# Rebuilding the opening of a fused cosformer attention and SwiGLU kernel: loads, order of the first heads, first FFN products

## The chip, the core and the metric

The kernel runs on one core of one Trainium2 chip. TensorE (PE) multiplies, with its weight loads (PEld) beside the products; VectorE (DVE), ScalarE (ACT) and GpSimd (POOL) do the elementwise work; SyncE (SP) and POOL issue most of the DMAs. The metric is device time in microseconds: 299.17 us in the median of three runs before the change (298.46 to 299.66). All times inside a run are counted from the start of its profiled span.

## What is computed

Linear attention with cosine weights feeds a gated FFN (cut to what matters):

```
# q, k, v: [8 batches, 8 heads, 576 positions, 64]; theta = pi/2 * pos / 576
phi(x) = concat(relu(x) * cos(theta), relu(x) * sin(theta))          # 128 features
kv  = einsum('bhsf,bhsd->bhfd', phi(k), v);   z = sum_s phi(k)
x   = (phi(q) @ kv) / (phi(q) @ z + 1e-6)                            # 4608 tokens x 512
g   = x @ w_gate;  val = x @ w_val                                   # 512 -> 1536
out = (g * sigmoid(g) * val) @ w_out                                 # 1536 -> 512
```

Inputs and output are fp32 in HBM; the kernel multiplies in bf16 and fp16.

## The kernel before

The 4608 tokens make 72 rows of 64 positions and so 36 token tiles of 128 (a tile is two such rows); four tiles make a token group, and nine groups go through the FFN one after the other. A batch of q, k or v is held as `[128, 4, 9, 64]`: 64 partitions for each of two heads, four groups `g` of two heads, nine slots `c`, 64 channels. The slot `c` of q belongs to one half of a token tile, so tile 0 needs slots 0 and 1, tile 1 slots 2 and 3, and so on, of all heads; k and v are needed whole, for all nine slots, before a head's `kv` is known.

Two regimes stand one behind the other.

- **The opening** treats batch 0 and the first half of the gate and value products of token group 0 (blocks `fc` 0 to 5 of 12). Its order is written out by hand in the string `words` (from L510), each word an instruction group that is put on its engine's queue in that order: `rk` relu of k, `kv` the product of k and v by pairs of head groups (`kv_first`, L315), `kvo` its eviction to SBUF, `tq` turning q on PE (`turn_q`, L351), `qr` relu of the turned q, `qw` its copy times tan(theta) (L360), `a` the product of q with kv for a token tile (`a_tile`, L372), `den`, `rec`, `x` the division (L388, L397, L401), `xt` and `xc` the turning of x on PE and its copy to `xT` (L418, L323), `G` and `V` the gate and value products (`ffn_mm`, L438), `s` silu (L445), `m` the product of the two (L450), `WG` and `WV` sums of weights that the later Strassen-like blocks use. A digit after the letter is a token tile or an `fc` block, what stands behind the point is the half (0, 1) or the pair of token tiles (01, 23). `z` puts products of zeros on PE.
- **The planned part** is everything after the words. Each piece of work is a `Job` with durations, dependencies and due times; a list scheduler (`order_once`) puts them in order at build time. Its inputs are constants: release times of loads (`LOADED`, `W_AT`, `WO_AT`), the moment at which each engine is taken to come free (`BUSY_AT`), and a list of seeds (`SEEDS`), one per 10 us of PE work, that shake the due times. Another seed gives another order of the same jobs.

Loads that bring fp32 to fp32 go through SP (`load_first`, L154) into space that is used for something else later: all of v into `wo_sb`, all of k into `ht`, the first two slots of q into `wt_sb`. They are issued at once, in the order v groups 0 and 1, v groups 2 and 3, q slots 0 and 1, k groups 0 and 1, k groups 2 and 3 slots 0 to 4, k groups 2 and 3 slots 5 to 8. ACT then makes bf16 of v (L461), ACT and DVE of q (L339), and the relu of k makes bf16 on the way (L281, L283). Loads that cast from fp32 to bf16 or fp16 go through POOL: q slots 2 and 3, q slots 4 to 7 (`load_slots`, L129), then the gate and value weights (`load_w`, L269 and L270) in blocks of `fc`: 0, 1, then pairs 2-3, 4-5, 6-7, then k of batch 1, and so on. POOL starts with them behind a one-column copy (`hold`, L467) that waits for the first half of v. Eight POOL loads can be outstanding; the ninth waits for the first to land.

Every PSUM result stands in one of eight banks, which `take` hands out and `give_back` frees.

Of the kernel before, what the change touches and what calls it, by code (L numbers as in the profile page):

```python
# [11 lines left out]
FP32 = mybir.dt.float32  # L12
# [7 lines left out]
def kernel(  # L20
# [112 lines left out]
    QCUT = 2  # L133
# [12 lines left out]

    first = {"q": lodge(G * QCUT * D, FP32).rearrange("p (g c d) -> p g c d", g=G, c=QCUT)}

# [15 lines left out]
    NW = 8  # L164
# [26 lines left out]
    idle_products(40, 16)  # L191
    idle_products(4)
# [30 lines left out]
    tan16 = consts.tile([P, NC + 1], FP16, name="tan16")  # L223
    eps_all = consts.tile([P, NC], FP32, name="eps")
    diag = lodge((NC + 1) * SH, FP16).rearrange("p (c s) -> p c s", c=NC + 1)
    tanT = consts.tile([P, NC + 1, SH], FP16, name="tanT")

    def tangents():
        nc.vector.reciprocal(out=rcos, in_=cs_all[:, :, :, 0])
        nc.vector.tensor_tensor(out=tan16[:, 0:NC], in0=csk[:, :, 1], in1=rcos[:, 0], op=ALU.mult)  # L230
        nc.vector.tensor_copy(out=tan16[:, NC:], in_=tan16[:, 0:1])
        nc.vector.tensor_single_scalar(out=eps_all, in_=rcos[:, 1], scalar=1e-6, op=ALU.mult)

    def tangent_diagonals():
        nc.vector.tensor_tensor(out=diag[0:SH], in0=ident16[0:SH, 0:SH].unsqueeze(1).to_broadcast([SH, NC + 1, SH]),
                                in1=tan16[0:SH].unsqueeze(2).to_broadcast([SH, NC + 1, SH]), op=ALU.mult)

    def tangents_spread():
        st["tan"] = take(2, "tan")
        nc.tensor.matmul(out=st["tan"][:, 0], lhsT=ones[0:SH], rhs=diag[0:SH, 0:NW].rearrange("p c s -> p (c s)"),  # L240
                         start=True, stop=True)
        nc.tensor.matmul(out=st["tan"][:, 1, 0:2 * SH], lhsT=ones[0:SH], rhs=diag[0:SH, NW:].rearrange("p c s -> p (c s)"),
                         start=True, stop=True)

    def tangents_out(eng):
        copy_op(eng, tanT.rearrange("p c s -> p (c s)"),
                st["tan"].rearrange("p b x -> p (b x)")[:, 0:(NC + 1) * SH])
        give_back("tan")
# [40 lines left out]
    def relu_first_k(g, eng, lo=0, hi=NC):  # L289
        relu_op(eng, raw_of(0, "k")[:, g, lo:hi], first["k"][:, g, lo:hi])  # L290

    def vmul(b, g):
        nc.vector.tensor_tensor(
            out=v2s[b == 1][:, g, :, :, 0:D],
            in0=(first if b == 0 and g == 0 else {"v": raw_of(b, "v")})["v"][:, g].unsqueeze(2).to_broadcast([P, NC, 2, D]),
# [29 lines left out]
    def kv_first_out(j, e, eng):  # L325
# [6 lines left out]
    qf = wgs_sb.rearrange("p n c u x -> p (n c u x)")[:, G * NC * 2 * W:G * NC * 2 * W + 4 * J * D].bitcast(  # L332
        BF16).rearrange("p (c j i d) -> p c j i d", c=2, j=J, i=2)
# [3 lines left out]
    def cast_q(c, eng):  # L337
        o = qf[:, c % 2].rearrange("p j i d -> p (j i) d")
        (nc.scalar.copy if eng == "act" else nc.vector.tensor_copy)(out=o, in_=first["q"][:, :, c])  # L339

    def turn_q(t):
        ps = take(1, ("tq", t)).bitcast(BF16).rearrange("p (y e s) -> p y e s", e=2, s=SH)
        for j in range(J):
            for c in range(2):
                y = 2 * j + c
                if t == 0:
                    nc.tensor.transpose(out=ps[:, y].rearrange("p e s -> p (e s)"),
                                        in_=qf[:, c, j].rearrange("p i d -> p (i d)"), identity=ident)
                    continue
# [16 lines left out]
    def a_tile(t, j):  # L366
# [3 lines left out]
        for e in range(2):  # L370
            for w in range(2):
                nc.tensor.matmul(  # L372
                    out=(ps[:, j, 2 * e * D1:2 * (e + 1) * D1] if t == 0 else
# [6 lines left out]
    def a_view(t, ps, ys):  # L380
        if t == 0:
# [3 lines left out]
    def x_den(t, ps, ys=slice(0, 4)):  # L385
        if ys.start == 0:
            st["den", t] = den_all[:, t % 4]
        nc.vector.tensor_scalar(  # L388
# [70 lines left out]
    for g in (0, 1, 2, 3):  # L459
# [3 lines left out]
        if g == 1:  # L463
            tangent_diagonals()
# [1215 lines left out]
```

## Time and profile before

| what | us |
|---|---|
| median of three runs | 299.17 (298.46 to 299.66) |
| the profiled execution, whole | 298.92 |
| its span, first to last instruction | 297.1 |
| PE busy in the span | 291.6 (98%) |
| DVE, ACT, POOL busy | 252.9, 199.4, 67.4 |
| first gate product (L438) starts | 16.10 |
| first product of the planned part (L904) starts | 27.41 |
| last stores issued | 293.17 |

PE's busy time contains 65 products of zeros (L187), 56 of them from 0.99 us on, so that its share says little on the first ten microseconds; the time of the opening is read from what each engine waits for, in the timeline. A line of the timeline is start and duration in us, engine, line, operation, output and input, shapes, count, and in brackets the idle time before it and what ended it.

### The profile page before, as it was taken

The numbers are of one execution on the slowest core, as the hardware profiler recorded it, in microseconds if no ns is written. First come the engines' busy times: TensorE is split into PE (matmuls) and PEld (weight loads), VectorE is DVE, ScalarE is ACT, GpSimd is POOL, SyncE is SP. The second block draws the span as 40 slices with busy tenths as digits, with TensorE's granted clock in tenths as the row PEclk, the third lists the DMA queues.
The fourth block names the chain that finished last, engine by engine and source line by source line (L and its number), as shares of the span: only waits on it lengthen the run. The fifth ranks groups of instructions, "written<-read, shape, count | busy, mean of one in ns | idle before, by whom it ended". The sixth has DMA issues, their size and how long they took to land.

```text
span 297.1 us, 8071 instructions
## 1 busy us (share of the span) xinstructions
PE 291.6 (98%) x3244; PEld 238.9 (80%) x3244; DVE 252.9 (85%) x514; ACT 199.4 (67%) x421; POOL 67.4 (23%) x122
## 2 busy tenths in 40 slices
PE   8999999999999999999999999999999999999994
PEld 4597465776787888898898889888988988888883
DVE  8878997879877999999888997998679868986883
ACT  6564346989559968975699589967465556565630
POOL 6763630003006022220352023200220050002000
PEclk9999999999999999999999999999999999999999
DMA  7999999997989998799996969950460045002025
GB/s 259 232 196 198 202 206 207 199 220 122 190 163 146 226 189 122 148 171 149 159 213 128 196 106 169 163 100 2 109 107 2 0 83 132 2 0 73 0 59 156
DMA packets 71973, 40.89 MB, mean 138 GB/s; under 512 B 48768, under 2 KB 68736, under 8 KB 71936
## 3 DMA queue, kind: packets, MB, share of 16 engines
q0 software_dynamic: 24800, 24.39, 48.9%
q1 hardware_dynamic: 46528, 15.47, 28.9%
q10 hardware_dynamic: 608, 0.52, 0.6%
q8 instruction: 25, 0.41, 0.6%
q14 instruction: 12, 0.10, 0.1%
HBM read 37.75 MB, written 9.44 MB: 159 GB/s over the span
## 4 chain that ended last, share of the span: by engine, by line
PE 94%; DMA 1%; DVE 1%; SPq 1%; issue 1%; ACT 0%
PE banks L977 44%; PE banks L1142 23%; PE banks L1052 5%; PE banks L1262 4%; PE banks L438 4%; PE banks L904 4%; PE banks L187 3%; PE banks L716 2%; PE banks L785 2%; DMA xT<-x 1%; SPq L747 1%; PE banks L779 1%; PE banks L372 1%; PE banks L1310 0%; PE banks L315 0%
## 5 line engine op out<-in xcount | busy, mean ns | idle before, releaser
L1111 POOL DMA_DIRECT2D out_dram<-ob x52 | 27.5, 536 | 105.3 <-ACT ob L630 70.0
L1036 ACT ACTIVATE sg<-banks 128x512 bf16<-128x512 f32 x72 | 41.3, 599 | 5.8 <-PE banks L977 5.6
L977 PEld LDWEIGHTS <-wg_sb 128*128 128x128 f16 x384 | 36.9, 98 | 6.6 <-DMA xT<-x 0.4
L628 ACT COPY banks<-banks 128x512 f32<-128x512 f32 (+1 forms) x53 | 29.9, 572 | 17.7 <-PE banks L1142 6.5
L1142 PEld LDWEIGHTS <-ht 128*128 128x128 f16 x384 | 37.5, 98 | 4.9
L1072 DVE TENSOR_TENSOR ht<-sg,banks 128x512 f16<-128x512 bf16 x60 | 39.9, 680 | 0.8 <-PE banks L977 0.6
L977 PEld LDWEIGHTS <-wgs_sb 128*128 128x128 f16 x368 | 35.8, 98 | 4.5
L997 DVE TENSOR_TENSOR banks<-m,banks 128x512 f32<-128x512 f32 x44 | 30.2, 693 | 10.5 <-ACT m L628 8.4
L977 PEld LDWEIGHTS <-wv_sb 128*128 128x128 f16 x320 | 31.1, 98 | 3.7
L977 PE MATMUL banks<-kvt,wgs_sb 128*128 128x256 f16 x236 | 33.4, 273 | 0.0
L1142 PEld LDWEIGHTS <-sums 128*128 128x128 f16 x288 | 27.9, 98 | 3.4
L630 ACT ACTIVATE ob<-banks 128x512 f32<-128x512 f32 x32 | 18.8, 596 | 15.9 <-PE banks L1142 15.2
L977 PE MATMUL banks<-xT,wg_sb 128*128 128x256 f16 x192 | 28.8, 273 | 0.1
L628 ACT COPY m<-banks 128x512 f32<-128x512 f32 x44 | 25.5, 590 | 4.4 <-PE banks L977 4.3
L1142 PE MATMUL banks<-wo_sb,ht 128*128 128x256 f16 x192 | 25.7, 273 | 0.0
L1142 PE MATMUL banks<-wt_sb,sums 128*128 128x256 f16 x192 | 24.9, 273 | 0.0
L977 PE MATMUL banks<-xT,wv_sb 128*128 128x256 f16 x160 | 24.0, 273 | 0.0
L1036 ACT ACTIVATE sg<-m 128x512 bf16<-128x512 f32 x24 | 15.1, 630 | 12.3 <-DVE m L1005 12.1
L807 DVE TENSOR_TENSOR x<-banks,rec 128x512 f16<-128x512 f32 x32 | 21.6, 686 | 1.6 <-DVE rec L803 0.3
L977 PE MATMUL banks<-kvt,wg_sb 128*128 128x256 f16 x168 | 22.4, 273 | 0.0
L1142 PE MATMUL banks<-wt_sb,ht 128*128 128x256 f16 x192 | 22.3, 272 | 0.0
L877 ACT ACTIVATE r_q<-raw_q,tanq 128x256 bf16<-128x256 bf16 x45 | 20.7, 510 | 0.0
(160 smaller groups left out, 543.8 us busy)
## 6 DMA issues: line engine op xcount, KB each, us to landing
out_dram<-ob POOLq DMA_DIRECT2D x52, 128.0 KB, 4.0
raw_kv<-in_k_dram POOLq DMA_DIRECT2D x7, 576.0 KB, 5.9
raw_q<-in_q_dram POOLq DMA_DIRECT2D x12, 288.0 KB, 10.4
raw_kv<-in_v_dram POOLq DMA_DIRECT2D x6, 576.0 KB, 8.4
out_dram<-ob SPq DMA_DIRECT2D x12, 128.0 KB, 2.6
wg_sb<-in_moe_w_gate_dram POOLq DMA_DIRECT2D x5, 256.0 KB, 8.6
wv_sb<-in_moe_w_val_dram POOLq DMA_DIRECT2D x5, 256.0 KB, 9.2
wo_sb<-in_v_dram SPq DMA_DIRECT2D x2, 576.0 KB, 4.2
```

Source lines behind the costliest of these rows:

```text
L438: nc.tensor.matmul(out=st["f", tg, fc, lo][i], lhsT=(wg_sb, wv_sb)[i][:, kc, fs], rhs=xT[tg][:, ts, kc], start=(kc == 0), stop=(kc == KC - 1))
L628: nc.scalar.copy(out=out, in_=in_)
L630: nc.scalar.mul(out=out, in_=in_, mul=mul)
L807: tt(out=one(x_all, x).rearrange("p (y e d) -> p e y d", e=2, d=D), in0=view()[:, :, :, 0:D], in1=rec_all[:, t % 4].rearrange("p (e y) o - ...
L877: nc.scalar.activation(out=home()[:, :, c, 1], in_=raws[b, "q"][:, :, c], func=AF.Relu, scale=tanq[:, c:c + 1])
L977: nc.tensor.matmul(out=to[:, i], lhsT=a[:, c, 2 * u + i], rhs=x()[:, :, c], start=first and i == 0 and c == 0, stop=c == KH - 1, skip_grou ...
L997: tt(out=bank(c), in0=one(m7_all, m).rearrange("p i x -> p (i x)"), in1=bank(b), op=ALU.add)
L1036: nc.scalar.activation(out=gates(rooms[w])[:, :, jh * HT:(jh + 1) * HT], in_=src, func=AF.Silu, scale=DOWN)
L1052: nc.tensor.matmul(out=bank(v), lhsT=wv_sb[:, kc, fc * P:(fc + 1) * P], rhs=xT[tg][:, :, kc], start=(kc == 0), stop=(kc == KC - 1))
L1072: tt(out=ht[:, 4 * u + w:4 * u + w + 3:2, jh * HT:(jh + 1) * HT], in0=gates(rooms[w])[:, :, jh * HT:(jh + 1) * HT], in1=src.rearrange("p ( ...
L1111: {"POOL": nc.gpsimd, "SP": nc.sync, "ACT": nc.scalar}[j.eng].dma_start(out=out_v[idx // NC, idx % NC][:, cols], in_=ob_of(t)[e * SH:(e + ...
L1142: nc.tensor.matmul(out=to, lhsT=a[:, kc, i * P:(i + 1) * P], rhs=b[:, kc], start=first and kc == 0 and i == 0, stop=kc == HC - 1, skip_gro ...
```

## The change

- **Loads.** SP loads only groups 0 and 1 of v and of k as fp32, two transfers. POOL has no `hold`; it issues at once, all casting, q slots 0 to 3, v groups 2 and 3, k groups 2 and 3 slots 0 to 4, the same slots 5 to 8, q slots 4 to 7, and then the weights as before. The fp32 room for q, its casts (`cq`) and the branch of `turn_q` for tile 0 are gone; the ACT cast of v is done for groups 0 and 1 alone.
- **Zero products.** 12 at the start in place of 12 + 40 + 4, and one later group of 3 in place of 4 + 2 + 1 + 2.
- **Tangents.** The diagonals are built on 128 partitions with 320 columns (`eye2`, `tan5`) and no longer on 64 with 640; `epd_all` is made there and not in the planned part.
- **Order.** Heads of groups 0 and 1 go first: `kv` of pair 0, then `a0.0` and `a1.0`, the first halves of token tiles 0 and 1, through den, rec and x, before `kv` of pair 1 is complete. Tile 1 is laid out in halves as tile 0 was (`HALVED`). All `den` are put on ACT. One relu of turned q changes its engine, and `xc2` goes to DVE.
- **FFN.** Token tiles 0 and 1 are multiplied together (256 columns); the first gate and value blocks are split by the contraction: `Gl`, `Vl` take the first 256 channels of x (heads of pair 0), `Gh`, `Vh` the rest.
- **Planned part.** Release times 400 ns later, DVE free at 600 and not 750, new seeds, and the four stores of two token tiles of the last group but one go through POOL and not SP.

```diff
-    QCUT = 2
+    NW, QCUT = 8, 4
-    first = {"q": lodge(G * QCUT * D, FP32).rearrange("p (g c d) -> p g c d", g=G, c=QCUT)}
+    first = {}
     KCUT = 5
     load_first("v", slice(0, 2))
-    load_first("v", slice(2, 4))
-    load_first("q", slice(0, G), 0, 2)
     load_first("k", slice(0, 2))
-    load_first("k", slice(2, 4), 0, KCUT)
-    load_first("k", slice(2, 4), KCUT, NC)
     idle_products(12)
-    idle_products(40, 16)
-    idle_products(4)
...
     def tangent_diagonals():
-        nc.vector.tensor_tensor(out=diag[0:SH], in0=ident16[0:SH, 0:SH].unsqueeze(1).to_broadcast([SH, NC + 1, SH]),
-                                in1=tan16[0:SH].unsqueeze(2).to_broadcast([SH, NC + 1, SH]), op=ALU.mult)
+        nc.vector.tensor_tensor(out=diag, in0=eye2.unsqueeze(1).to_broadcast([P, NH2, SH]),
+                                in1=tan5.unsqueeze(2).to_broadcast([P, NH2, SH]), op=ALU.mult)
+        nc.vector.tensor_tensor(out=tan16, in0=csk[0:SH, :, 1], in1=rcos[0:SH, 0], op=ALU.mult)
...
     def relu_first_k(g, eng, lo=0, hi=NC):
-        relu_op(eng, raw_of(0, "k")[:, g, lo:hi], first["k"][:, g, lo:hi])
+        o = raw_of(0, "k")[:, g, lo:hi]
+        relu_op(eng, o, first["k"][:, g, lo:hi] if g < 2 else o)
...
-    def x_den(t, ps, ys=slice(0, 4)):
+    def x_den(t, ps, ys=slice(0, 4), eng=""):
...
+        if eng == "act":
+            nc.scalar.activation(out=o, in_=i_, func=AF.Identity, scale=DOWN, bias=epd_all[:, 2 * t:2 * t + 1])
...
-    def ffn_mm(tg, fc, lo=0, hi=GH, which=(0, 1)):
+    def ffn_mm(tg, fc, lo=0, hi=GH, which=(0, 1), ks=range(KC)):
...
-            for kc in range(KC):
+            for kc in ks:
...
+    def load_part(nm, gs, lo, hi):
+        nc.gpsimd.dma_start(out=raw_of(0, nm)[:, gs, lo:hi].rearrange("p g c d -> p g (c d)"),
+                            in_=source(0, nm)[:, gs, lo * D:hi * D])
     tangents()
-    for g in (0, 1, 2, 3):
-        if g:
-            nc.scalar.copy(out=raw_of(0, "v")[:, g], in_=first["v"][:, g])
-        vmul(0, g)
-        if g == 1:
-            tangent_diagonals()
-    nc.gpsimd.tensor_copy(out=hold, in_=first["v"][:, 1, 0, 0:1])
-    load_slots(0, "q", QCUT, 4)
-    load_slots(0, "q", 4, NW)
+    load_part("q", slice(0, G), 0, QCUT)
+    load_part("v", slice(2, 4), 0, NC)
+    load_part("k", slice(2, 4), 0, KCUT)
+    load_part("k", slice(2, 4), KCUT, NC)
+    load_part("q", slice(0, G), QCUT, NW)
     load_w(0, 1)
     load_w(1, 1)
...
     words = """
-        tm0 te0@act cq1@act cq0@dve z4 rk1.0@dve rk0.0@act rk3.0@dve rk2.0@dve tq0 z2 rk3.1@dve kv0.0 qr0@act
-        kv1.0 qw0.1 rk2.1@act kvo01@dve kv1.1 tq1 kvo00@act kvo10@dve a0.0 kvo11@act qr1@dve z1 den0.0 qw1.1
...
+        vc0@act td0 vm0 rk0.0@dve tm0 z3 tq0 vc1@act vm1 qr0@dve te0@act rk1.0@act kv0.0 qw0.1 kvo01@act tq1 vm2 qr1@dve kvo00@act qw1.1 a0.0 rk3.0@act den0.0@act rk2.0@act a1.0 vm3 rk2.1@dve den1.0@act rec0.0 rk3.1@act rec1.0 x0.0 kv1.0 kv1.1 x1.0 tq2 ld0 kvo11@dve kvo10@act tq3 a0.1 xt0.0 a1.1 qr3@act xc0.0@act qr2@dve qw2.1 xt1.0 den1.1@act den0.1@act qw3.1 xc1.0@act rec1.1 a2.0 rec0.1 x1.1 a2.1 den2@act a3.0 a3.1 x0.1 xt1.1 rec2 xt0.1 Gl0.01 xc1.1@act xc0.1@act den3@act x2.0 Vl0.01 G1.01 rec3 Gh0.01 V1.01 Vh0.01 x3.0 G3.01 xt2.0 xt3.0 G2.01 V2.01
...
-    LOADED = {("k", 1): 440.0, ("v0", 1): 7580.0, ("v1", 1): 9080.0, ("sa", 1): 10080.0, ("sb", 1): 14480.0, ("q", 2): 22280.0,
+    LOADED = {("k", 1): 840.0, ("v0", 1): 7980.0, ("v1", 1): 9480.0, ("sa", 1): 10480.0, ("sb", 1): 14880.0, ("q", 2): 22680.0,
...
-                store_jobs(t, [e11] + e12, [rooms[0]], ("SP", "SP") if tg == NTG - 2 else ("POOL", "POOL"))
+                store_jobs(t, [e11] + e12, [rooms[0]], ("POOL", "POOL"))
...
-    BUSY_AT = {"PE": 0.0, "ACT": 0.0, "DVE": 750.0, "POOL": 0.0, "SP": 0.0}
+    BUSY_AT = {"PE": 0.0, "ACT": 0.0, "DVE": 600.0, "POOL": 0.0, "SP": 0.0}
...
-    SEEDS = (51094, 66641, 10020, 27923, 14121, 98735, 44165, 18236, 50235, 79911, 24891, 60631, 13014, 94291, 24750, 63675, 71408, 99473, 46185, 48516, 52068, 68761, 26309, 0, 39492, 83147, 0, 0)
+    SEEDS = (49757, 92194, 0, 93731, 10715, 42893, 64891, 49657, 99755, 71336, 35271, 27776, 63066, 66391, 0, 20410, 23048, 69833, 11363, 84271, 96830, 68068, 65144, 13506, 39926, 0, 0, 0)
```

More of the change, by code (lines that the diff above doesn't have):

```diff
@@ L294, in vmul @@
             out=v2s[b == 1][:, g, :, :, 0:D],
[L295 removed]
+            in0=(first["v"] if b == 0 and g < 2 and g not in cast_v else raw_of(b, "v"))[:, g].unsqueeze(2).to_broadcast([P, NC, 2, D]),
             in1=tab, op=ALU.mult,
@@ L429, in ffn_mm @@
         fs = slice(fc * P, (fc + 1) * P)
-        if 0 in which:
+        if 0 in which and 0 in ks:
             if 2 * n <= 512:
@@ L521 @@
             done_early.add((op[1], a, part))
-        elif op == "cq":
-            cast_q(a, eng)
+        elif op == "ld":
+            loads()
+        elif op == "vc":
+            copy_op(eng, raw_of(0, "v")[:, a], first["v"][:, a])
+            cast_v.add(a)
+        elif op == "vm":
+            vmul(0, a)
         elif op == "tq":
@@ L557 @@
             span = (2 * tiles[0], 2 * tiles[-1] + 2)
-            if op in "GV":
-                ffn_mm(0, a, *span, which=("GV".index(op),))
+            if op[0] in "GV":
+                ffn_mm(0, a, *span, which=("GV".index(op[0]),),
+                       ks={"l": range(KC // 2), "h": range(KC // 2, KC)}.get(op[1:], range(KC)))
             elif op == "s":
@@ L799, in fn @@
                 nc.vector.tensor_scalar(out=o, in0=i_, scalar1=eps_all[:, c0:c0 + 1], scalar2=DOWN, op0=ALU.add, op1=ALU.mult)
-        den = Job(DEN_ON, fn, after=[mm] + J_["eps"], put=[r])
+        den = Job(DEN_ON, fn, after=[mm], put=[r])
         def fn(j):
```

112 lines of the change are left out of this document (50 added, 62 removed).

## The prediction

> **What bounds the kernel now.** I read the page first, then the span by stages, then the timeline of the opening. From the page and the stage table (columns: PE, PEld, DVE, ACT, POOL busy, clock, DMA share, GB/s):
>
> ```profile
> span 297.1 us, 8071 instructions
> ...
> PE 291.6 (98%) x3244; PEld 238.9 (80%) x3244; DVE 252.9 (85%) x514; ACT 199.4 (67%) x421; POOL 67.4 (23%) x122
> ...
> 0.00:10.10 10.10, 9.05 (x68) 4.13 (x69) 8.03 (x24) 6.43 (x10) 7.52 (x20) 1.00 0.88 272
> 10.10:16.04 5.94, 5.93 (x139) 4.39 (x138) 5.53 (x20) 3.38 (x9) 4.02 (x6) 1.00 1.63 188
> 16.04:27.30 11.26, 11.26 (x128) 10.25 (x126) 8.31 (x26) 5.96 (x17) 5.46 (x8) 1.00 1.39 199
> 27.30:292.90 265.60, 265.36 (x2916) 220.17 (x2913) 230.57 (x446) 183.61 (x386) 50.38 (x90) 1.00 0.75 129
> ```
>
> From 16.04 to 292.90 PE is busy all but 0.24 us, so that stretch can lose time easily and gain little. What stands between PE products there is a second view, the waits of the weight loads after 16 us:
>
> ```profile
> PEld L693 <- DVE ht L924: 0.4, 1, 0.4
> PEld L716 <- ACT m L628: 0.4, 1, 0.4
> ...
> PEld L977 <- DMA xT<-x: 0.4, 1, 0.4
> PEld L977 <- DVE x L807: 0.3, 1, 0.3
> ```
>
> These four, 1.5 us, are all it waits for others. The rest of the kernel is bound by PE's own work, and the change can win only what the first 16 us take. There the timeline shows a chain of landings:
>
> ```profile
> 4.41 0.67 ACT L461 CAST raw_kv<-wo_sb 128x576 bf16<-128x576 f32 x1
> ...
> 5.94 1.25 ACT L461 CAST raw_kv<-wo_sb 128x576 bf16<-128x576 f32 x2 [0.86 <-DMA wo_sb<-in_v_dram]
> ...
> 9.53 1.58 DVE L283 TENSOR_SCALAR raw_kv<-ht 128x576 bf16<-128x576 f32 x3 [0.71 <-DMA ht<-in_k_dram]
> ...
> 11.34 0.42 ACT L281 ACTIVATE raw_kv<-ht 128x256 bf16<-128x256 f32 x1 [0.64 <-DMA ht<-in_k_dram]
> ...
> 11.88 0.83 DVE L323 CAST kvt<-banks 128x260 bf16<-128x260 f32 x2
> ...
> 13.29 0.64 PE L351 MATMUL banks<-ident,raw_q 128*64 128x128 bf16 x16
> ...
> 13.77 0.74 DVE L401 TENSOR_TENSOR x<-banks,rec 128x256 f16<-128x256 f32 x2
> ...
> 15.08 0.65 ACT L323 COPY xT<-banks 128x256 f16<-128x256 f16 x2 [0.24 <-PE banks L418]
> ...
> 16.10 0.38 PE L438 MATMUL banks<-xT,wg_sb 128*128 128x128 f16 x4
> ...
> 17.68 0.75 POOL L270 DMA_DIRECT2D wv_sb<-in_moe_w_val_dram  x1 [0.56 <-DMA wg_sb<-in_moe_w_gate_dram]
> ...
> 21.66 0.74 POOL L270 DMA_DIRECT2D wv_sb<-in_moe_w_val_dram  x1 [0.60 <-DMA wv_sb<-in_moe_w_val_dram]
> ...
> 27.41 1.03 PE L904 MATMUL banks<-xT,wv_sb 128*128 128x512 f16 x4
> ```
>
> v lands in halves (4.41, 5.94), the last of k at 11.34, q slots 4 to 7 at 13.29; both kv are evicted at 12.71 (11.88 + 0.83), the first gate product starts at 16.10, and the planned part takes over between 27.30 and 27.41, say 27.35. Only waits for the landings end idle time of ACT and DVE here; PE fills its own with products of zeros.
>
> **Part 1, the loads.** Sizes come from the page (KB written):
>
> ```profile
> wo_sb<-in_v_dram SPq DMA_DIRECT2D x2, 576.0 KB, 4.2
> ...
> wg_sb<-in_moe_w_gate_dram POOLq DMA_DIRECT2D x5, 256.0 KB, 8.6
> ...
> q1 hardware_dynamic: 825, 1.10, 102.4%
> ```
>
> The last row is the queue list between 5.9 and 8.9 us, all of it: SP's queue alone; POOL's first loads, issued behind `hold` once v had landed at 4.41, move nothing in those 3 us. The new SP pair, half of v and half of k, has the sizes and issue places of the two v halves, so they land at 4.41 and 5.94: k groups 0 and 1 come 3.6 us earlier than at 9.53. Behind them, in KB read: q 512, v 576, k 320, k 256, q 512, in all 2176, exactly what lies between 5.94 and 13.29 before (q 256, k 576, 320, 256, q 256 and 512). Two rates bound it. Fast: POOL's waits between 17.68 and 21.66 are three landings of weights of 256 KB written, 512 read, in 3.98 us: 385 KB per us. Slow: before's own stretch, 2176 KB in 7.35 us, 296. Fast, the last k lands at 10.26 and the last q at 11.59; slow, at 11.56 and 13.29. The new set has no small q transfers and no change of queue in its middle, the old stretch has the same total: I take the middle, 10.9 and 12.4. POOL issues the five at about 0.75 us each (the row at 17.68), 3.8 us in all, and starts before 4.41, where `hold` let it go: ahead of the data.
>
> **Part 2, from the last k to the first FFN product.** Before, the last k to both kv in SBUF takes 12.71 - 11.34 = 1.37 us, by the same operations as after: 12.3. What DVE then does before the first product of the FFN can be fed:
>
> ```profile
> L360 DVE TENSOR_TENSOR wt_sb<-wt_sb,tanT 128x512 bf16<-128x512 bf16 x4 | 1.6, 406 | 0.0
> ...
> L235 DVE TENSOR_TENSOR wt_sb<-ident,tan 64x640 f16<-64x640 f16 x1 | 0.8, 809 | 0.0
> ...
> L388 DVE TENSOR_SCALAR den<-banks,eps 128x4 f32<-128x4 f32 x2 | 0.4, 216 | 0.0
> L283 DVE TENSOR_SCALAR wt_sb<-banks 128x512 bf16<-128x512 bf16 x1 | 0.4, 421 | 0.0
> ...
> L397 DVE RECIPROCAL rec<-den 128x4 f32<-128x4 f32 x2 | 0.3, 174 | 0.0
> ```
>
> After: relu of q 0.42, two weightings 0.81, two reciprocals 0.3, two half x at 0.37 each (13.77 row), together 2.3 us, and 0.3 for the turning: first FFN product at 14.9, against 16.10. The first halves of tiles 0 and 1 are made earlier, while k of groups 2 and 3 is on its way; DVE has room there, for ACT now makes most of k's relus and the cast of q is gone. The dens, six of 0.22, go to ACT, which loses one v cast (0.67) and a q cast; as they lie behind copies there they can cost up to 0.4 before x1.1, counted in the 2.3 only by its rounding. The diagonals (0.81 on DVE) become half as wide and are finished ahead of any landing: nothing. `hold` did nothing but delay POOL; its removal is Part 1.
>
> **Part 3, the FFN half of group 0.** Column work is the same. Prices:
>
> ```profile
> 18.17 0.27 PEld L418 LDWEIGHTS <-x 128*128 128x128 f16 x4
> ...
> 18.67 1.91 PE L438 MATMUL banks<-xT,wg_sb 128*128 128x256 f16 x16
> ```
>
> 16 products of 256 columns in 1.91 us with about 0.17 of tail are 0.109 each. 6 blocks x 2 x 2 x 4 = 96 of them are 10.5 us, two turns of x at 0.27 make 0.5, and the gap between `Gl`, `Vl` (4 products, 0.44) and `G1`, which waits for two copies of 0.33 on ACT, about 0.3. So 14.9 + 11.3 = 26.2, 1.15 us ahead of 27.35. But `G3.01`, 16 products later at 14.9 + 1.75 + 0.3 = 16.95, needs weights that landed at 17.68 before. With the last q 0.9 earlier they come at 16.8; unmoved, they cost 0.75. I take half, 0.35, as with the rates: **the opening gains 0.8 us**. Bounds: all fast, 1.8; all slow (k 0.66 later, weights unmoved), 0.4; and 0 if also ACT's dens hold x back.
>
> **Part 4, zero products and bank waits.** 44 + 6 fewer stand where PE has nothing on the path: nothing, as long as the clock stays up (rival 2).
>
> **Part 5, the planned part.** Its jobs are the same; new seeds reorder them. I take 0, between -1.5 (the four waits above gone) and +1.5 (as much again). The release times only steer the order at build time. The four stores moved to POOL:
>
> ```profile
> out_dram<-ob POOLq DMA_DIRECT2D x52, 128.0 KB, 4.0
> ...
> out_dram<-ob SPq DMA_DIRECT2D x12, 128.0 KB, 2.6
> ...
> 286.52 2.40 SPq L1111 DMA_DIRECT2D out_dram<-ob  x4
> ...
> 293.17 1.16 ACTq L1249 DMA_DIRECT2D out_dram<-r_q  x2
> ```
>
> At 4.0 instead of 2.6 us those issued at 286.5 to 288.9 land by 293, before the last pair is even issued: nothing; without that cover at most 1.4. SP's own stores behind them, from 289 on, lose a queue of 2.40 ahead of them and wait for data anyway.
>
> **The sum.** Profiled 298.92 - 0.8 + 0 = 298.1. The median of the runs lies 0.25 above that execution (299.17), so I predict 298.4.
>
> **Rivals.** 1. *The bytes bind.* Same KB behind 5.94, so the last k and the weights land as before and the regrouping only fills waiting time: first product at 14.9 + 0.66, then `G3.01` held to 17.68; opening gains 0 to 0.4, time 299.0. For it: the DMA share 0.88 and 1.63 in both opening rows, nothing idle. Against it: the fast rate of the same kind of load. The Trainium skill (DMA: Bandwidth & Descriptors, Issuing engines are not separate DMA queues) says that transfers of SP and POOL run on the same 16 engines, and moving issue from one to another saves only issue time; by that rule this rival holds. The equal byte count agrees, the two rates 296 and 385 do not.
>
> 2. *The clock falls, and it gets slower.* Products of zeros kept PE busy; after, PE waits in pieces from about 7 to 15 us. The trace shows what a thin stretch does at the end, in slices of 3.41 us:
>
> ```profile
> 292.23:295.64 3.41, 0.71 (x7) 0.39 (x4) 0.85 (x2) 0.00 (x0) 0.00 (x0) 1.00 0.84 228
> 295.64:297.10 1.46, 0.00 (x0) 0.00 (x0) 0.00 (x0) 0.00 (x0) 0.00 (x0) 0.51 0.00 0
> ...
> 2.67 0.15 PEld L187 LDWEIGHTS <-zeros 128*128 128x128 bf16 x1 [0.28 <-issue]
> ...
> 8.35 1.04 PE L187 MATMUL banks<-zeros 128*128 128x512 bf16 x4
> ```
>
> After a stretch with PE busy 21% the granted clock is 0.51. At the start a product of zeros takes 0.43 us (weight loads 2.67, then 3.10), at 8.35 about 0.22. If the clock falls near 12 us and rises near 19, two such stretches, the 4 us of products there take twice as long, of which waiting hides about half: +2 us, 300.4. It decides if busy shares of 50 to 70%, which I count for these stretches, are too little; the trace has only 21% (down) and full (up). The Trainium skill (TensorE: Matmul & The Clock Gate, Part 1: The HAM clock gate) lets the clock fall after an idle window of about 3.4 us; by that rule it stays up here, as no window is idle. The trace's 21% was not quite idle and fell.
>
> 3. *The new seeds decide*: a stall more or less of 1.2 us in the planned part, 299.6 or 297.2.
>
> **How the numbers follow.** Forecast 0.58, its own range 297.7 to 298.9; bytes bind 0.17; clock 0.10; seeds 0.15, half on each side. A measurement of this kernel tells about 0.5% (1.5 us) from no change. Faster than 297.7: a fifth of the forecast's weight (the fast bound) and the good seeds, 0.2. Slower than 300.7: half of the clock rival (with slow loads on top) and part of the bad seeds, 0.1. Range 297.0 to 300.4 takes in the fast bound with even seeds and the clock.
>
> **What would show it.** Relu of k on DVE at 6.0; the last k's relu between 10.3 and 11.6; first product of the FFN (256 columns) near 15; planned part from 26.2 to 27; granted clock without a dip between 9 and 19 us; no new PE wait over 0.5 us behind 30 us. A first FFN product at 16 or later, or weight loads that wait for `wg_sb` at `G3.01`, make the gain wrong; products at 0.22 us per 256 columns would be the clock.

## The result, and the profile after

The changed kernel takes 301.97 us (median of six executions, 300.89 to 303.98), the kernel before, run beside it, 298.90 (298.27 to 299.93): 1.0114 times as long, 95% interval 1.0087 to 1.0142. It is slower by 3.1 us, and 1.6 us beyond the upper end of the predicted range. The profiled execution took 302.3 us, with a span of 300.5.

The page after, its busy line, and the span by the same stages as before (columns: PE, PEld, DVE, ACT, POOL busy, clock, DMA share, GB/s):

```profile
span 300.5 us, 7946 instructions
...
PE 290.1 (97%) x3182; PEld 236.7 (79%) x3182; DVE 249.3 (83%) x510; ACT 198.8 (66%) x425; POOL 71.9 (24%) x128
...
PE 75%; DMA 17%; DVE 4%; ACT 1%; POOL 1%; issue 1%; POOLq 0%; ACTq 0%; DVEq 0%; SPq 0%
```

The last of these lines is the chain of work that ended last, by engine; before, it was:

```profile
PE 94%; DMA 1%; DVE 1%; SPq 1%; issue 1%; ACT 0%
```

The stages:

```profile
10.10:16.04 5.94, 5.21 (x97) 3.89 (x97) 5.57 (x19) 4.29 (x15) 5.30 (x8) 1.00 1.63 187
16.04:27.30 11.26, 11.22 (x106) 9.72 (x104) 7.77 (x22) 5.18 (x17) 4.90 (x7) 1.00 1.39 199
27.30:292.90 265.60, 262.45 (x2889) 217.60 (x2887) 226.51 (x439) 183.35 (x387) 52.98 (x94) 1.00 0.73 127
292.90:300.50 7.60, 2.84 (x26) 2.30 (x24) 2.14 (x6) 0.00 (x0) 0.00 (x0) 1.00 0.53 148
```

The opening is not where the time went: no stage of this execution shows a lower clock, and the planned part starts earlier than before (26.93 against 27.41, below). Between 27.30 and 292.90 PE is busy 262.45 us and not 265.36: 2.9 us of idle time are new there, products are left over for the last stage, and the chain of work that ended last now runs 17% over DMA and not 1%.

The opening, in its timeline:

```profile
11.19 0.75 DVE L295 TENSOR_TENSOR v<-raw_kv,tab 128x1152 bf16<-128x1152 bf16 x1
...
11.86 0.45 DVE L282 TENSOR_SCALAR raw_kv<-raw_kv 128x256 bf16<-128x256 bf16 x1
...
12.44 0.75 DVE L393 TENSOR_TENSOR x<-banks,rec 128x256 f16<-128x256 f32 x2
...
13.11 0.42 DVE L325 CAST kvt<-banks 128x260 bf16<-128x260 f32 x1
...
15.79 0.38 PE L431 MATMUL banks<-xT,wg_sb 128*128 128x256 f16 x2
...
26.93 1.03 PE L894 MATMUL banks<-xT,wg_sb 128*128 128x512 f16 x4
```

The last k landed at 11.16 (the semaphore of its load), but DVE took it at 11.86, behind the last v (11.19), and evicted the last kv at 13.11 + 0.42 = 13.53, behind two x (12.44). The first FFN product starts at 15.79, the planned part at 26.93: the opening gains 27.41 - 26.93 = 0.48 us.

What PE waits for between 27.3 and 292.9. Before, the same question gives no line at all; after:

```profile
PE banks L967 <- DMA xT<-x: 1.4, 1, 1.4
PE banks L967 <- DVE banks L987: 1.4, 1, 1.4
PE banks L967 <- ACT kv L623: 0.2, 1, 0.2
PE banks L775 <- DVE x L797: 0.2, 1, 0.2
```

The first is at 74.59. PE needs the second token tile of group 2, turned by a DMA transpose that SP issues. SP's queue, POOL's queue and the DMA view of this place, before:

```profile
67.88 1.19 SPq L747 DMA_TRANSPOSE xT<-x  x1
...
68.87 0.75 POOL L121 DMA_DIRECT2D raw_kv<-in_k_dram  x1 [0.40 <-ACT m L628]
...
xT<-x SPq DMA_TRANSPOSE x1, 2.4
```

and after, with the DMA queues between 68.5 and 70.5:

```profile
67.90 1.19 SPq L737 DMA_TRANSPOSE xT<-x  x1
...
68.33 0.75 POOL L121 DMA_DIRECT2D raw_kv<-in_k_dram  x1 [0.40 <-ACT sg L1026]
...
xT<-x SPq DMA_TRANSPOSE x1, 6.6
...
q8 instruction: 1, 0.02, 4.5%
```

The transpose is issued at the same moment and lands after 6.6 us instead of 2.4. Two things differ: POOL's casting loads of batch 3 follow it after 0.43 us and not 0.99, and a DMA of 16 KB on the queue marked "instruction" runs in the same time. Before, that one starts at 64.3 (the row between 64 and 65.5 us):

```profile
q8 instruction: 1, 0.02, 4.6%
```

By the semaphore, which counts the parts of 16 DMA engines, 15 had done their part of the transpose in the changed kernel at 72.14, the last at 74.46.

The second stall is at 91.75. DVE's timeline there:

```profile
87.37 0.41 DVE L940 TENSOR_TENSOR kvt<-xT,kvt 128x512 f16<-128x512 f16 x1
90.27 0.83 DVE L282 TENSOR_SCALAR r_q<-raw_q 128x1152 bf16<-128x1152 bf16 x2 [2.49 <-DMA phit<-r_q]
91.01 0.69 DVE L987 TENSOR_TENSOR banks<-m,banks 128x512 f32<-128x512 f32 x1
```

Two relus of q may overwrite their space only when the transpose of phi has read it (landed 90.14; before, 87.84). DVE takes its work in order: it sits idle for 2.49 us before them, and the sum that PE waits for (L987) stands behind them. The transpose of phi came later because it was issued later: SP issues the fourth transpose of the group 3.09 us after the third (1.39 before), and that of phi behind it at 75.35 and not 73.47. What held SP there is not shown.

### The profile page after: what moved, and what is told of

It is laid out like the page before. It is cut to its first block, busy times and chain, and to the rows that moved or that the text cites. A ratio compares the mean times of both kernels' runs of the same rounds, so it can differ in the third digit from the quotient of the medians.

```text
span 300.5 us, 7946 instructions
## 1 busy us (share of the span) xinstructions
PE 290.1 (97%) x3182; PEld 236.7 (79%) x3182; DVE 249.3 (83%) x510; ACT 198.8 (66%) x425; POOL 71.9 (24%) x128
## 4 chain that ended last, share of the span: by engine, by line
PE 75%; DMA 17%; DVE 4%; ACT 1%; POOL 1%; issue 1%; POOLq 0%; ACTq 0%; DVEq 0%; SPq 0%
PE banks L967 38%; PE banks L1132 18%; DMA phit<-r_q 9%; DMA raw_kv<-in_v_dram 5%; PE banks L1252 4%; PE banks L431 4%; PE banks L894 3%; DMA xT<-x 2%; PE banks L1042 2%; PE banks L775 2%; PE banks L706 2%; PE banks L769 1%; DVE x L797 1%; PE banks L364 1%; DVE v L295 1%
## 5 line engine op out<-in xcount | busy, mean ns | idle before, releaser
L1101 POOL DMA_DIRECT2D out_dram<-ob x56 | 29.3, 533 | 123.0 <-ACT ob L625 97.5
L987 DVE TENSOR_TENSOR banks<-m,banks 128x512 f32<-128x512 f32 x44 | 30.3, 692 | 10.7 <-ACT m L623 6.6
L967 PE MATMUL banks<-kvt,wgs_sb 128*128 128x256 f16 x236 | 34.2, 272 | 0.2 <-ACT kv L623 0.2
L1132 PE MATMUL banks<-wt_sb,sums 128*128 128x256 f16 x192 | 24.1, 273 | 0.0
L295 DVE TENSOR_TENSOR v<-raw_kv,tab 128x1152 bf16<-128x1152 bf16 x28 | 20.4, 749 | 0.5 <-DMA raw_kv<-in_v_dram 0.4
```

Source lines behind the costliest of these rows:

```text
L295: nc.vector.tensor_tensor(out=v2s[b == 1][:, g, :, :, 0:D], in0=(first["v"] if b == 0 and g < 2 and g not in cast_v else raw_of(b, "v"))[: ...
L967: nc.tensor.matmul(out=to[:, i], lhsT=a[:, c, 2 * u + i], rhs=x()[:, :, c], start=first and i == 0 and c == 0, stop=c == KH - 1, skip_grou ...
L987: tt(out=bank(c), in0=one(m7_all, m).rearrange("p i x -> p (i x)"), in1=bank(b), op=ALU.add)
L1101: {"POOL": nc.gpsimd, "SP": nc.sync, "ACT": nc.scalar}[j.eng].dma_start(out=out_v[idx // NC, idx % NC][:, cols], in_=ob_of(t)[e * SH:(e + ...
L1132: nc.tensor.matmul(out=to, lhsT=a[:, kc, i * P:(i + 1) * P], rhs=b[:, kc], start=first and kc == 0 and i == 0, stop=kc == HC - 1, skip_gro ...
```

## The experiments

Each kernel was run beside the kernel before, whose medians were 298.6 to 298.9. "Order" is the list that the planner makes of the planned part; in the experiments it is written out, so that it stays when something else is changed. A kernel is named by the short sign that stands ahead of its diff or its number (e1b, t_f).

### Opening and order exchanged

The diff of the first pair: the planner's call is replaced by a list `job:engine:banks` taken from the other kernel, with the eight PSUM banks renamed to those that the opening leaves free first.

> The changed opening (loads, zero products, words, half blocks) in front of the planned part in exactly the order, engines and banks of the kernel before; the four stores go through SP again. Theory P (the order that the new seeds gave the planned part loses about 3.5 us, the opening gains about 0.5): 298.4, ratio to before 0.997 to 1.000, and neither of the two PE stalls of over 1 us at 74.6 and 91.8. Rival O (the changed opening itself loses the time, by what it leaves to the planned part: later loads, DVE behind, or a lower clock): 301 to 302, ratio 1.007 to 1.011, with the stalls.

> The opening of the kernel before in front of the planned part in the order, engines and banks of the changed kernel. Theory P: about 302.4, ratio 1.010 to 1.014, with the two stalls at about 75 and 92. Rival O: 299, ratio 0.998 to 1.002.

Measured: e1 337.39 us (1.128) and e2 323.05 (1.080). Neither theory gives such times; the renaming was at fault, as the repetition without it shows. Tiles of two banks had stood on neighbours, and after the renaming they had banks of others between them. That PE therefore waited for the readers of banks that it did not write fits its waits (eleven for x alone in the first) and was not tested by itself. Nothing follows on the change. The pair was repeated with the banks as planned:

```
-    {0: 4, 4: 0, 5: 6, 7: 5, 2: 7, 1: 2, 6: 1, 3: 3}   (bank names)
+    (as planned)
```

> As the first try of the changed opening in front of the planned order of the kernel before, but with the PSUM banks as the planner gave them, so that tiles of two banks stand on neighbours. Theory P (the new order of the planned part loses the time): 298.4, ratio to before 0.997 to 1.000. Rival O (the opening itself loses it): 301 to 302. Theory F (each order fits the landing and issue times of its own opening, and any exchange loses): over 300, with stalls of over 1 us at other places than 75 and 92.

> The opening of the kernel before in front of the planned order of the changed kernel, banks as its planner gave them. Theory P: 302.4 (ratio 1.010 to 1.014), with the stalls near 75 and 92. Rival O: 299, ratio 0.998 to 1.002. Theory F: over 300, with stalls elsewhere.

Measured: e1b, new opening with old order, 306.88 us, ratio 1.0233 (1.0189 to 1.0276); e2b, old opening with new order, 299.62, ratio 1.0030 (1.0012 to 1.0048). My theory P, that the new order loses the time, falls: alone it costs 0.8 us. The new opening costs 8 us with the old order and some 2.4 with the new one, though in both it starts the planned part earlier (27.14 and 26.93 against 27.41). In the profiled execution with the new order and the old opening, DVE does the same two relus without a long wait, since the transpose of phi landed at 88.30:

```profile
88.42 0.85 DVE L285 TENSOR_SCALAR r_q<-raw_q 128x1152 bf16<-128x1152 bf16 x2 [0.44 <-DMA phit<-r_q]
89.53 0.70 DVE L994 TENSOR_TENSOR banks<-m,banks 128x512 f32<-128x512 f32 x1 [0.26 <-ACT m L630]
```

### The two stalls

```
e5  -  batch_loads(lambda: xT[2][0:1, 0, 0, 0:2], [J_["xT", 8]], names)
    +  batch_loads(lambda: xT[2][0:1, 1, 0, 0:2], [J_["xT", 8]], names)
e6     order on DVE: the two r_q relus behind the next seven DVE jobs
e9  -  nc.gpsimd.tensor_copy(out=hold2, in_=read())
    +  (the same copy four times, for batch 3)
e10    e6 and e9 together
```

> The changed kernel, its planned order kept; only the copy on POOL that holds back the loads of batch 3 reads the second turned x tile and not the first, so that these loads are issued after the transpose that PE waits for at 74.6 has landed. Theory T1 (the casting loads overtake that transpose): it lands in about 2.5 us and not 6.6, the stall of 1.4 us is gone, time 300.6 (ratio to before about 1.006). Rival (the transpose is slow by itself, or the loads, later by 2 us, are missed): the stall stays or another takes its place, time 302.

> The changed kernel, its planned order kept but for two relus of q on DVE (which wait for the transpose of phi to have read what they overwrite), put seven DVE jobs later, behind the products that PE waits for at 91.8. Theory T2 (DVE takes its work in order, so the two relus hold up work that is ready): the stall of 1.4 us is gone, time 300.6 (ratio about 1.006). Rival (the stall has another releaser, or the relus, now later, hold up the next turning of q): 302.

> The changed kernel with one edit: the copy on POOL ahead of the loads of batch 3 is made four times and not once, so that these loads are issued some 0.5 us later. Theory R (a race of two queues: the transpose at 67.90 takes SP 1.19 us to issue, to 69.09, and the first load takes POOL 0.75 from 68.33, to 69.08; the one issued first goes first): the transpose lands in 2.5 us, the stall at 74.6 is gone, and what follows it, the transpose of phi issued 1.9 us later than before, is earlier too; 300.0 to 300.6 (ratio 1.004 to 1.006). Rival (the transpose is slow for another reason): the stall stays, 302.

> The delayed loads of batch 3 together with the two relus of q put behind the seven DVE jobs. Theory R and T2 (two stalls of 1.4 us, each with its own cause): 299.0 to 299.6 (ratio 1.000 to 1.003), no PE wait of over 1 us after 20 us. If the second stall only follows the first: the same as with the delayed loads alone. If the gaps are not what the time hangs on: 301 to 302.

Measured: e5, loads behind the second tile, 304.52 (1.0169); e6, relus moved, 301.15 (1.0075, 1.0046 to 1.0105); e9, loads half a microsecond later, 303.23 (1.0147); e10, both together, 299.64 (1.0036, 1.0014 to 1.0058). With the loads behind the second tile the transpose landed in 3.6 us and the first stall went, but everything that needs the loads was late, and a new stall of 1.8 us took its place (ACT waited 2.29 us for k and PE for a copy behind it), while the second grew from 1.4 to 1.7: the rival written there, at a higher price. Delaying the loads alone did not help either: in that execution x came later too, the loads still followed after only 0.31 us, and the transpose took 5.5 us, to 74.0. PE, later as well, needed the tile at 73.8, so that 0.3 us are left of the first stall, but the second grew to 2.1 us. Moving the relus alone takes away 0.8 us; its profiled execution, the fastest of nine (299.65), has no PE wait behind 27 us at all. Both edits together take away 2.3 of the 3.1 us, with two of thirteen executions at 305.6 all the same. So most of the time hangs on the stalls; how large each is differs from execution to execution, so that the share of each is not shown.

### The moment of the handover, and the stores

```
x1a    words of the changed kernel + " z2"
x1b    words of the changed kernel + " z4"
x5     words of the kernel before  + " z4"
xs  -  store_jobs(t, [e11] + e12, [rooms[0]], ("POOL", "POOL"))
    +  store_jobs(t, [e11] + e12, [rooms[0]], ("SP", "SP") if tg == NTG - 2 else ("POOL", "POOL"))
```

> The changed kernel, its planned order kept, with two products of zeros (0.43 us) on PE between the opening and the planned part, so that the opening's gain of 0.48 us is given away. Theory S (the new opening costs by the moment at which the planned part starts: shifted, transposes and bulk loads meet in another order): the two stalls at 75 and 92 go, 299.5 to 300.5. Rival L (the opening leaves something else behind, such as queues or a lower clock, or the stalls belong to the order): the stalls stay, 302.2 to 302.8.

> The same with four products of zeros (0.86 us). Theory S: as with two, or again other stalls: 299.9 to 301. Rival L: 302.6 to 303.2.

> The kernel before, its planned order kept, with four products of zeros (0.86 us) between its opening and its planned part. If a shift alone brings stalls (theory S, for any order): 301 or more, with PE waits of over 1 us after 30 us. If not: 299.7 to 299.9, which is the delay alone.

> The changed kernel, its planned order kept, with the four stores of the last group but one through SP's queue again, as in the kernel before. The prediction put their move at nothing: 302.0 then, the same as the changed kernel within 0.3. If the move holds up the last stores: 301.3 to 301.6, by an end that comes 0.5 us sooner behind the last product.

Measured: x1a 303.19 (1.0142), x1b 303.11 (1.0114), x5 299.34 (1.0038, 1.0017 to 1.0058) and xs 303.67 (1.0177). Giving the opening's gain away brings nothing back (in the profiled executions the planned part starts at 27.79 in x1a and 27.71 in x1b), and the kernel before pays for the delay alone: it has no PE wait behind 27 us even then. Theory S falls. Stalls come with the new opening wherever it hands over; with two products of zeros:

```profile
PE banks L967 <- DMA xT<-x: 2.7, 1, 2.7
```

The stores are not the cause; through SP again it is not faster. Whether the 1.7 us by which xs lies above the changed kernel come from the four stores or from runs at another time was not separated; a difference of that size between kernels that were not run together proves little.

### The products of zeros

What the new opening has less of, whenever it hands over, is PE instructions: 3182 products after and 3244 before, each with its weight load, so 62 x 2 = 124 fewer. PE's instructions come by DMA. The page after has, among its queues:

```profile
q8 instruction: 25, 0.41, 0.6%
```

25 transfers of 16 KB for 6364 PE instructions, one per 255. The Trainium skill (Runtime: NRT & Kernel Launch, Instruction fetch mechanics) says the same: blocks of 16 KiB, 256 instructions, which the engine's sequencer fetches over a DMA queue of its own. It adds that crossing a block is mostly hidden. The trace agrees on the block. What is hidden from PE need not be hidden from another transfer: with 124 instructions fewer, each later fetch meets other work. In the changed kernel the one at 69.0 meets the transpose.

```
t_b -  idle_products(12)
    +  idle_products(11), then 40 products of 4 columns; word z3: 25 of 4 columns
t_c -  idle_products(12)
    +  idle_products(17)
t_a -  idle_products(40, 16); idle_products(4); ... z4      (kernel before)
    +  idle_products(2);      idle_products(1); ... z1
t_d    new opening, old order (as e1b), and the edit of t_b
```

> The changed kernel, its planned order kept, with 61 more products of zeros in the opening, of 4 columns each (76 in place of 15, 122 PE instructions more, some 1.7 us of PE time in place of four long products), so that PE's instruction fetches fall on the same work as in the kernel before. Theory I (the removed products moved PE's instruction fetches, and one of them now falls on the transpose at 68): the fetch at 69.0 comes at 63 to 65, the transpose lands within 4 us on all engines, the stalls at 75 and 92 go; 299.0 to 300.0. Rival L (anything else in the opening): 301.5 to 303.

> The changed kernel, its planned order kept, with 5 more long products of zeros at the start (1.1 us or more of PE time, 10 PE instructions): the activity of the kernel with tiny products without its shift. Theory I: the fetch stays at 68 to 69, 301.5 to 303. Rival C (PE's activity in the opening, by the clock): 299 to 300.

> The kernel before, its planned order kept, with 44 fewer products of zeros in the opening (88 PE instructions), which brings its fetch at 64.3 to about 68.5. Theory I: the transpose issued at 67.9 gets one late engine, and stalls of over 1 us come behind 74; 300.5 to 302.5. Rival: 298.6 to 299.2, if neither the fetch nor the missing products cost anything.

> The changed opening with the planned order of the kernel before (306.9) and with the 61 tiny products. Theory I: 298.2 to 299.0, the gain of the opening (0.5) kept. Rival L: 305 to 308.

Measured, all four outside the ranges that theory I had written: t_b, tiny products, 302.44 (1.0106, 1.0082 to 1.0129); t_c, long products, 303.60 (1.0153), so rival C falls, and the fetch stays at 69.2; t_a, the kernel before with 44 fewer, 300.10 (1.0029, 1.0010 to 1.0048), smaller than I wrote, but four of its twelve executions took 301.1 to 305.6; t_d, new opening with old order and tiny products, 299.62 (1.0037, 1.0012 to 1.0061), where without them it took 306.88. In the changed kernel the tiny products took the first stall from 1.4 to 0.2 us and left the second at 1.7. But they did something else too. The opening of t_b, by windows:

```profile
4.06:7.47 3.41, 3.01 (x72) 2.08 (x70) 2.63 (x8) 2.31 (x4) 3.41 (x6) 1.00 1.18 258
7.47:10.88 3.41, 3.06 (x57) 2.16 (x58) 1.84 (x4) 1.09 (x4) 3.41 (x6) 0.50 1.29 182
```

The granted clock fell to 0.50, and the planned part began at 27.70. Products of four columns count as PE work and did not hold the clock. So the same number of instructions was put back in the form that the kernel before has.

### The same instructions, as products of 64 columns

```
-  idle_products(12)                         word z3
+  idle_products(8), then 67 of 64 columns   word z1
```

> The changed opening and the planned order of the kernel before, with 61 more products of zeros in the opening: 8 long and 67 of 64 columns at the start in place of 12 long, and 1 long in place of 3 later. Theory I with the clock held: first FFN product at 15.5 to 16.1, no PE wait of over 1 us behind 30 us, 298.0 to 298.7 (ratio 0.997 to 1.000). If the fetches explain only part of what the exchange cost: 300 or more, with stalls.

> The changed kernel with its own planned order and the same products of zeros in the opening. Theory I: the PE fetch that came at 69.0 comes at 64 to 66, the transpose issued at 68 has no late engine, the stall at 75 is under 0.5 us; the one at 92 stays if the fetch near 88 falls on the end of the transpose of phi. 299.3 to 300.8 (ratio 1.002 to 1.007). Rival: 302, with both stalls as they are.

Measured: t_f, new opening with old order, 299.28 us, ratio 1.0015 (1.0000 to 1.0031); t_g, changed kernel, 301.11, ratio 1.0062 (1.0038 to 1.0085). Against e1b and the changed kernel, the first edit is worth 7.6 us, the second 0.9. The 0.9 alone would prove little, since the two were not run together, but the ratio of t_g lies below those of all kernels with this order and about as few products (after, x1a, x1b, xs and t_c: 1.0114 to 1.0177). The times of t_f and t_g are above the ranges written for them, by 0.6 and 0.3 us. One rival is left for the 7.6: the planned part starts at 28.20 in t_f and at 30.11 in t_d, where e1b has 27.14, and a later start was tested with the new order (x1a, x1b) and with the old opening (x5), not with this pair. In both the transpose lands as before, in t_g:

```profile
xT<-x SPq DMA_TRANSPOSE x1, 2.4
...
q8 instruction: 1, 0.02, 5.8%
```

the first row for 68 to 69 us, the second for 64.5 to 66, where the fetch now is. No stall at 75 is left in either. The second stays in t_g, as written (2.7 us in the profiled execution): the transpose of phi has one late engine (88.64, the last at 90.17) beside a fetch at 87.9. The opening's gain is not kept by t_f: with a fetch at 12.3 the load of the last q, then under way, is late on one engine (14.32; in the changed kernel 12.57), and the planned part starts at 28.20. No version beats the kernel before.

### The transpose at 68 in all of them

From the semaphores of the profiled executions (us): how long after the transpose the loads were issued, when 15 engines and when the last had done their part, counted from its issue, and where PE's fetch was. The profiled execution is one of many: those of t_a (305.2), t_g (303.8) and e10 (305.6) took longer than nearly all others of their kernels, those of e1b (303.6) and e6 (299.7) were the fastest.

| kernel | loads after | 15 engines | last | PE's fetch at |
|---|---|---|---|---|
| t_g | 1.54 | 2.40 | 2.41 | 64.7 |
| before | 0.99 | 2.39 | 2.40 | 64.3 |
| t_f | 0.90 | 2.41 | 2.41 | 65.3 |
| x5 | 0.83 | 2.39 | 2.39 | 65.6 |
| t_d | 0.46 | 3.91 | 3.96 | 67.5 |
| t_b | 0.15 | 5.06 | 5.39 | 65.3 |
| e2b | 0.05 | 5.92 | 5.93 | 65.4 |
| t_a | 0.04 | 8.80 | 9.65 | 68.0 |
| e5 | 4.26 | 3.62 | 3.63 | 69.1 |
| e1b | 1.00 | 2.40 | 4.40 | 69.5 |
| e10 | 0.98 | 3.62 | 3.65 | 69.0 |
| e6 | 0.66 | 3.46 | 3.96 | 69.5 |
| after | 0.43 | 4.24 | 6.56 | 69.0 |
| t_c | 0.44 | 4.10 | 6.47 | 69.2 |
| xs | 0.43 | 4.19 | 6.51 | 68.9 |
| e9 | 0.31 | 4.11 | 5.51 | 69.5 |
| x1b | 0.26 | 4.69 | 6.47 | 69.9 |
| x1a | 0.13 | 5.82 | 7.94 | 69.8 |

Two things add up. The smaller the lead of the transpose over the bulk loads, the later most engines are: 2.4 us from a lead of 0.8 on, if no fetch is near, and 3.9 to 8.8 below 0.5. And a single engine that is late by 1.4 us or more (up to 2.4) appears in seven of the ten executions with a fetch at 68.9 to 69.9, and in none of the eight with the fetch earlier.

The lead is 0.99 before and 0.43 after, but it is no property of the order alone: with the old order it is 0.04 to 1.00, with the new one 0.05 to 1.54 without e5, e9 and e10, which hold the loads back. The fetch goes by the number of PE instructions ahead. PE needs the tile 73.2 - 67.9 = 5.3 us after its issue in the changed kernel: with 4.24 it would not have waited, with 6.56 it did.

In this table, fetch and late engine are a coincidence in time. The same 18 traces hold a wider sample. Beside 80 of their transposes of x no packet of POOL's loads starts, from 0.5 us before the issue to the end. Where a fetch of PE starts in the 2.4 us after the issue (23 of the 80), the last engine is done after 2.69 to 4.50 us, where none does (57), after 2.39 to 2.64. So a fetch delays a transpose without any load, and mostly on all engines alike, as in e5 and e10 in the table (3.6 us in spite of a long lead). The single engine that is late by 1.4 us or more occurs in none of these 80. Among the transposes with loads beside them it is there in 18 of 77 with a fetch that starts 0.9 to 2.4 us after the issue, and in 3 of the other 347; the kernel before has such a case itself, at 139.09 (15 engines after 2.49 us, the last after 4.29, a fetch 2.24 us and the loads 1.53 us behind the issue). By which step in the DMA engines this comes about is not shown.

Left open: in e1b the profiled execution was the fastest of its six (303.58; the median is 3.3 us above), so that I can show only a part of what it loses, a wait of 2.3 us for another transpose at 145.62, issued 0.49 us ahead of loads (138.47) where t_f has 1.34. After that wait one window of 3.4 us is at half clock, and the executions of e1b have mean clocks of 0.985 to 0.996, so that windows at half clock are part of its loss. And t_g keeps 2.2 us over the kernel before; its profiled execution (303.76, above its median) shows the second stall with 2.7 us and one of 0.7. What the others wait for was not recorded.

## Why the prediction was wrong

- **What bounds the kernel.** That PE's stretch from 16 to 293 us "can lose time easily and gain little" was right, and the loss is there. I then looked for the loss elsewhere.
- **Part 1, the loads.** Right. The last k landed at 11.16 (10.9 predicted, 10.26 to 11.56), the last q at 12.57 (12.4), the weights of the pair 2-3 at 16.84 (16.8). The 2176 KB behind the two transfers of SP (6.12) took 6.45 us, 337 KB per us, the middle of the two rates.
- **Part 2, from the last k to the first FFN product.** "12.71 - 11.34 = 1.37 us, by the same operations as after: 12.3" was mis-sized: 1.37 us became 13.53 - 11.16 = 2.37, since DVE had the last v and both x of pair 0 ahead of the eviction. I had put those x ahead of the last k, "while k of groups 2 and 3 is on its way". The 2.3 + 0.3 us that follow took 15.79 - 13.53 = 2.26, so the first FFN product came 0.9 us later than I wrote. (That only landings end idle time of ACT before the change was misread as well: its 1.06 us ahead of 13.75 end with a product of PE, which itself waits for q.)
- **Part 3, the FFN half.** 11.3 us predicted, 26.93 - 15.79 = 11.14 measured; the weights held PE once for 0.3 us, as half-priced. So the opening gained 0.48 us and not 0.8, inside the bounds, and close to the 0.4 of the slow side.
- **Part 4, zero products.** "nothing, as long as the clock stays up" failed. They are also PE instructions, and 124 fewer of them move every later fetch. Putting them back was worth 0.9 us in the changed kernel (302.0 against 301.1) and 7.6 with the old order, there with the rival of the later start.
- **Part 5, the planned part.** "Its jobs are the same; new seeds reorder them. I take 0", with 1.5 us to each side, is the step that failed: up to the start of its last product the planned part is longer by 3.3 us (268.53 against 265.26), 2.7 of them in two PE waits. It was treated as a block with a price of its own. By itself the new order costs 0.8; its worst parts, the short lead at 68 and the relus ahead of L987, become stalls only together with what the opening changed. I could have read the lead (0.99) and the 2.4 us of the transpose in the trace of before, and at 139.09 one that a fetch and loads make late. The stores moved to POOL cost nothing, as said; the 0.6 us by which the end is farther from the last product were not taken apart.
- **Rivals.** The bytes bound less than the first rival said: the last q came at 12.57 (13.10 before) and the weights at 16.84 (17.39), though the last k, at 11.16, hardly earlier than before (11.31). The clock did not fall in the profiled execution, and the busy share of 50 to 70%, by which I wanted to decide it, does not decide: in e9 PE was busy 2.10 of 3.44 us, and the next window is at half clock; in the changed kernel it was busy 2.43 of 3.42 us and the clock stays; but in t_g 2.00 of 3.41 (10.67 to 14.08) and in t_f 1.79 of 3.42 (12.75 to 16.17), and it stays too. The rule of the Trainium skill that I weighed there (TensorE: Matmul & The Clock Gate, Part 1: The HAM clock gate), a fall after an idle window, is too mild for e9: its window was not idle. Three of the six executions of the changed kernel have a mean clock of 0.989 to 0.992 and are at 301.6 to 304.0, so a part of the spread is windows at half clock; the other three, at 0.997 to 1.000, took 300.9 to 302.3, so that the clock is not what makes it slower. Two windows in the opening, the first pair of e9, the single one of the changed kernel:

```profile
7.70:11.14 3.44, 2.10 (x57) 1.39 (x53) 2.49 (x6) 1.50 (x5) 2.98 (x5) 1.00 1.32 184
11.14:14.55 3.41, 3.41 (x62) 2.65 (x63) 2.55 (x8) 1.47 (x5) 2.83 (x5) 0.50 1.75 180
```

```profile
6.98:10.40 3.42, 2.43 (x59) 1.44 (x58) 1.97 (x4) 1.66 (x4) 2.79 (x5) 1.00 1.19 171
```

  The third rival, the seeds, had the right place and 1.2 us; it got a chance of 0.15, half of it on the good side. What I had said would be absent, a new PE wait of over 0.5 us behind 30 us, is what came.

## What to carry to other kernels

Where the planned part of a kernel is full, price a change at its beginning by what it moves behind it: read every transfer that an engine waits for soon after its issue, how far the next bulk load is behind it, and where the engines' instruction fetches fall. Instructions that do no work are still fetched; taking them out (or putting some in) is a change of its own and wants a run of its own, with the number of instructions kept. An order made for one opening should be measured again with another, in both directions, before either is blamed.

## What was not expected of the hardware

- A DMA transpose of 2.4 us takes 3.9 and more when casting loads of another queue are issued less than 0.5 us after it, as in the table; on top, one of 16 engines was late by 1.4 to 2.4 us in seven of ten executions in which PE's 16 KB fetch ran at that time. Without any load, a fetch that starts in the 2.4 us after the issue makes 2.7 to 4.5 us of 2.4 to 2.6.
- A long PE stall costs more than its length. In e10's profiled execution (305.6 us, far above its median) PE waited 3.0 us for ACT, up to 121.15:

```profile
117.90:121.10 3.20, 0.24 (x3) 0.07 (x1) 1.71 (x3) 3.15 (x8) 1.13 (x2) 0.87 0.67 89
121.10:124.50 3.40, 3.35 (x16) 2.31 (x16) 0.70 (x1) 3.30 (x9) 0.00 (x0) 0.50 1.20 206
124.50:127.90 3.40, 3.40 (x22) 2.50 (x20) 0.69 (x1) 0.89 (x3) 0.00 (x0) 0.62 0.34 57
127.90:131.30 3.40, 3.40 (x45) 3.11 (x43) 3.38 (x7) 3.30 (x7) 2.12 (x4) 1.00 0.48 123
```

  The clock was at half from 120.26 to 127.08, two windows of 3.41 us, and the 28 products from 121.15 on took 0.105 us longer each, another 2.9 us. After a wait of 4.0 us in t_a it was two windows too, after waits of 2.0 to 2.7 us in t_c, e9, e1b and t_g one, after one of 2.7 us in x1a none, and after those of up to 1.8 us none. What separates them is how a wait lies in the windows: in those ahead of a fall PE was busy 0.80 to 1.40 us of 3.41, in all others of the planned part at full clock 1.68 or more; the wait of x1a lies across two (1.83 and 2.25). The Trainium skill (TensorE: Matmul & The Clock Gate, HAM oscillation — how this bites in real kernels) tells the same of waits over 3.4 us; here 2.0 were enough.
- Products of 4 columns do not hold the clock: in t_b PE counts as busy 3.01 of 3.41 us, and the next window is at 0.50, while 1.79 of 3.42 us of other products held it in t_f. In the opening, busy time is not what the clock goes by.
